# Convolution of the later groups in sixteen 32x32 TensorE tiles, with their loads, writes and reads in a new order

## The chip, the cores and the metric

One core of a Trainium2 chip runs the whole program. The metric is the device time in microseconds; the kernel before takes 413.99 us (median of three runs, 413.82 to 414.37). The engines of the core work side by side: TensorE (PE, with its weight loads as PEld) multiplies, VectorE (DVE) and ScalarE (ACT) work element by element, GpSimd (POOL) and SyncE (SP) mostly issue DMAs.

## What is computed

The input `x` has 8 sequences of 4160 tokens with 192 channels. First comes a causal convolution over 7 tokens, with softmaxed taps, one set for each of 8 heads of 24 channels. Then an RWKV channel mix: two blends of each token with the one before it, a hidden layer of 1024 with a squared relu, and a sigmoid gate.

```python
w = softmax(weight)                                   # (8 heads, 7 taps)
y[b, s, h, :] = sum over k of w[h, k] * x[b, s - 6 + k, h, :]      # zeros before the start

xk = mu_k * y + (1 - mu_k) * y_prev
xr = mu_r * y + (1 - mu_r) * y_prev                   # y_prev: one token earlier
k  = maximum(xk @ w_k, 0)                             # 192 -> 1024
out = sigmoid(xr @ w_r) * ((k * k) @ w_v)             # float32
```

## The kernel before

**Pairs, steps, bundles.** The eight sequences are worked on in four pairs. A pair runs through steps of 512 tokens (both sequences of a pair lie side by side on the partitions, 64 channels of one and 64 of the other, so three slices cover 192 channels). A step of 512 has eight slots of hidden work; four slots are a bundle, so a step takes two bundles. The first pair has bundles 0 to 15, the second 16 to 31, the third 32 to 47, the fourth 48 to 63, and the last 64 tokens of all sequences are gathered in bundle 64.

**The body of a bundle** (`bundle_rest`, line 861) is an order written out by hand. TensorE gets the k multiplies of two slots, a third slot, the r multiplies of a quad of tokens (`r`, line 594), half of the v multiplies (`v_rows`, line 625), the fourth slot, then the convolution units of the bundle, if it has any, and the other half of v. ScalarE evicts: relu of each slot (`k_relu`, line 549), sigmoid of r (line 605), casts of the convolution (line 319). VectorE squares the relu (line 563), blends (`diff`, `scale`, `add_y`), and multiplies v by r (`v_out`, line 641). All PSUM tiles come from one ring of four buffers of two banks each: each new tile takes the buffer of the fourth tile before it, and its first write waits until that tile has been read.

**The convolution ahead of it.** It is computed some bundles before its tokens are needed, in groups of blocks. `toe` is a banded 128x128 matrix for each head. Groups 0 to 3 of the first pair have a route of their own (`on_pe`). From group 4 on, a group has 10 blocks (the last one of a pair 8), each of 56 tokens on each of two partition halves, and a halo: `load_x` (line 116) brings 64 rows per half, batch and block with DMAs on POOL's queue, which cast to bf16. `conv_tiles` (line 288) multiplies two heads at a time: a 64x64 part of `toe` for input half i and output half j, eight multiplies of 5 x 2 x 24 = 240 columns (192 with 8 blocks) into one PSUM tile. `conv_tiles_out` (line 310) casts the tile to the y tile in SBUF, in one or two pieces. Four such units make a group, two units in each of two bundles, two bundles apart: `xs = [fb - 9] * 2 + [fb - 7] * 2` (line 694), where `fb` is the bundle of the step that needs the group first. So from bundle 15 to bundle 53 every second bundle has two units.

**Turning it.** At the end of the second of these bundles `y_write` (line 416) writes the y tile to HBM in four DMAs on SP's queue, and two bundles later `y_read` (line 429) reads the group back with one transposing DMA into `yT`, channels on partitions. `diff` of the step needs it in bundle `fb - 2`. SP's queue also carries the output, two DMAs per quad, and works in order: an instruction that waits holds up those behind it.

**Buffers.** x tiles (`xb`) rotate through three buffers of 10 blocks, y tiles through two, output tiles through three, `yT` through two (one for each pair in work). `x_tile` (line 103) puts a memset of one element on VectorE ahead of a load, so that POOL's DMA can't start before its place in VectorE's order.

Of the kernel before, what the change touches and what calls it, by code (L numbers as in the profile page):

```python
# [7 lines left out]
FP32 = mybir.dt.float32  # L8
BF16 = mybir.dt.bfloat16
# [5 lines left out]
def kernel(  # L15
# [11 lines left out]
    nc = tc.nc  # L27
# [11 lines left out]
    GB = 10  # L39
    HB = 56  # L40
    NROW = -(-S // (2 * HB)) * 2 * HB
    BANK = 512
# [46 lines left out]
    for p in range(NPAIR):  # L89
        base = 0  # L90
        for nb, s, on_pe in (
            ((3, 0, True), (4, 1, True), (4, 2, True), (5, 3, True), (10, 4, False), (10, 6, False))
            if p == 0
            else ((10, 0, False), (10, 2, False), (10, 4, False), (8, 6, False))
        ):
            groups.append((p, base, nb, first_bundle[first_step[p] + s], on_pe))
            base += nb * (BLK if on_pe else 2 * HB)
        assert S <= base <= NROW


    xbs = {}

    def x_tile(g):
        p, base, nb, _, on_pe = groups[g]
        xb = three.tile([P, GB, 2, D], BF16, tag="xb", name="xb")
        xbs[g] = xb
        if g > 4:

            nc.vector.memset(xb[0:1, 0, 0, 0:2], 0.0)  # L109
        if base == 0:  # L110
            nc.gpsimd.memset(xb[0:32, 0, :, :], 0.0)  # L111
        if not on_pe and base + 2 * nb * HB > S:
            n0 = nb - (base + 2 * nb * HB - S) // HB - 1
            nc.gpsimd.memset(xb[Q:P, n0:nb, :, :], 0.0)

    def load_x(g):
        p, base, nb, _, on_pe = groups[g]
        xb = xbs[g]
        if on_pe:
            parts, step, rows = ((0, base),), BLK, P  # L120
        else:
            parts, step, rows = ((0, base), (Q, base + nb * HB)), HB, Q
        for s in range(2):
            b = 2 * p + s
# [98 lines left out]
    def softmax():  # L223
        nc.vector.tensor_reduce(out=w_max, in_=w_raw, axis=mybir.AxisListType.X, op=ALU.max, negate=True)
        nc.scalar.activation(out=w_exp, in_=w_raw, func=AF.Exp, bias=w_max, accum_out=w_sum)
        nc.scalar.preload_act_table(AF.Sigmoid)
        xbs[0] = three.tile([P, GB, 2, D], BF16, tag="xb", name="xb")
        for c in range(NC):
            cs = slice(c * Q, (c + 1) * Q)
            nc.scalar.copy(out=xbs[0][:, : groups[0][2], :, cs], in_=x_f32[:, :, :, cs])  # L230
        nc.vector.reciprocal(out=w_sum, in_=w_sum)
# [78 lines left out]
    def conv_tiles_out(g, c):  # L310

        m = groups[g][2] // 2
        ps = conv_ps.pop((g, c))
        y = ys[g]
        c0, c1 = 2 * c * G, 2 * (c + 1) * G
        cuts = [c0] + [a for a in range(Q, D, Q) if c0 < a < c1] + [c1]
        for a, b in zip(cuts, cuts[1:]):
# [11 lines left out]
                ),  # L329
            )  # L330

    def conv_units(g):
# [83 lines left out]
    def y_write(g):  # L416
        p, base, nb, _, _ = groups[g]
        if base == 0:
            new_yT(p)
        m = nb // 2  # L420
        for j in range(2):
# [6 lines left out]

    def y_read(g):
        p, base, nb, _, _ = groups[g]  # L430
        r0, r1 = base, min(base + 2 * nb * HB, S)
        nc.sync.dma_start_transpose(
            out=yTs[p][:, :, YC + r0 : YC + r1], in_=y_drams[p][r0:r1, :]
        )
# [244 lines left out]
    def at(table, b, fn, *a):  # L679
        table.setdefault(b, []).append((fn, a))  # L680
# [7 lines left out]
    for g, (p, base, nb, fb, on_pe) in enumerate(groups):  # L688
        if g < 3:
            continue  # L690
        if p == 0:
            xs = {3: [1, 1], 4: [2, 2, 3, 3], 5: [4, 4, 5, 5]}[g]
        else:
            xs = [fb - 9] * 2 + [fb - 7] * 2
        for i, b in enumerate(xs):
            xt.setdefault(b, []).append((g, i))
        if not on_pe:
            at(late, xs[-1], y_write, g)

            at(mix_c if g == 4 else late, xs[-1] + (1 if g < 6 else 2), y_read, g)  # L700
# [55 lines left out]
    def prologue():  # L756
# [14 lines left out]
        nc.vector.memset(w_nrm, 0.0)  # L771
        nc.vector.memset(ones6, 1.0)
        x_tile(1)
        load_x(1)
# [86 lines left out]
    def bundle_rest(b, ns):  # L861
# [42 lines left out]
        for u in units:  # L904
            conv_tiles(*u)
            conv_tiles_out(*u)
        v_rows(*quad, 1)
# [85 lines left out]
```

## Time and profile before

The profiled execution has a span of 412.2 us from its first to its last instruction; the runs' median of 413.99 us is measured around it.

| What | Value |
|---|---|
| Median of three runs | 413.99 us |
| Span of the profiled execution | 412.2 us |
| Mean granted TensorE clock | 1.000 |
| k multiplies (line 537): busy | 191.0 us, x1632 |
| v multiplies (line 625): busy | 188.2 us, x4032 |
| r multiplies (line 594): busy | 43.1 us, x780 |
| convolution multiplies (line 302): busy | 16.6 us, x448 |
| relu on ScalarE (line 549): busy | 253.1 us, x260 |
| sigmoid on ScalarE (line 605): busy | 53.3 us, x65 |
| convolution casts on ScalarE (line 319): busy | 50.7 us, x84 |
| DMA moved | 65.58 MB, mean 159 GB/s |

Busy time is a share of the whole span and hides that stages have different limits; multiplies overlap each other, so the busy times of the groups of TensorE add up to more than the engine's own. What a multiply costs is read better from when the next one starts. The chain of waits is followed back from the last instruction: for each piece it gives start, length, engine, tile and line. The waits view tells for each engine what ended its idle time. A view of windows counts the instructions that overlap each stretch of time.

### The profile page before, as it was taken

The numbers are of one execution on the slowest core, as the hardware profiler recorded it, in microseconds if no ns is written. First come the engines' busy times: TensorE is split into PE (matmuls) and PEld (weight loads), VectorE is DVE, ScalarE is ACT, GpSimd is POOL, SyncE is SP. The second block draws the span as 40 slices with busy tenths as digits, with TensorE's granted clock in tenths as the row PEclk, the third lists the DMA queues.
The fourth block names the chain that finished last, engine by engine and source line by source line (L and its number), as shares of the span: only waits on it lengthen the run. The fifth ranks groups of instructions, "written<-read, shape, count | busy, mean of one in ns | idle before, by whom it ended". The sixth has DMA issues, their size and how long they took to land.

```text
span 412.2 us, 16799 instructions
## 1 busy us (share of the span) xinstructions
PE 403.7 (98%) x7349; PEld 301.7 (73%) x7350; DVE 370.5 (90%) x672; ACT 353.2 (86%) x426; POOL 64.1 (16%) x100
## 2 busy tenths in 40 slices
PE   7899999999999999999999999999999999999996
PEld 5567767767867777776777777777777777777795
DVE  5999799999999998999999999999989898999973
ACT  6899978889988888988888899888889888787781
POOL 8622023022040201104040110304000000000000
PEclk9999999999999999999999999999999999999999
DMA  9999989959978894998769697897863926321223
GB/s 141 192 200 194 191 200 190 253 133 194 198 110 211 151 214 118 200 218 113 198 121 229 156 196 182 111 226 130 188 163 100 184 82 175 107 67 53 80 80 115
DMA packets 137241, 65.58 MB, mean 159 GB/s; under 512 B 87356, under 2 KB 137168, under 8 KB 137168
## 3 DMA queue, kind: packets, MB, share of 16 engines
q1 hardware_dynamic: 95840, 48.42, 44.9%
q0 software_dynamic: 40528, 15.53, 33.0%
q8 instruction: 57, 0.93, 0.9%
q10 hardware_dynamic: 800, 0.57, 0.4%
q14 instruction: 16, 0.13, 0.1%
HBM read 31.62 MB, written 37.09 MB: 167 GB/s over the span
## 4 chain that ended last, share of the span: by engine, by line
PE 88%; DMA 4%; DVE 3%; ACT 2%; issue 1%; POOL 1%; SPq 0%; POOLq 0%
PE ps_v L625 39%; PE ps_k L537 37%; PE ps_r L594 7%; PE ps_c L302 3%; DMA yT<-y_dram 2%; DMA wk<-in_moe_w_k_dram 2%; DVE k L563 1%; PE ps_v L577 1%; DMA y_dram<-y 1%; ACT k_sb L549 1%; ACT y L319 0%; DVE d L480 0%; POOL xb L136 0%; DVE xr L511 0%; SPq L424 0%
## 5 line engine op out<-in xcount | busy, mean ns | idle before, releaser
L549 ACT ACTIVATE k_sb<-ps_k 128x1024 bf16<-128x1024 f32 x260 | 253.1, 1037 | 36.1 <-PE ps_k L537 35.2
L563 DVE TENSOR_TENSOR k<-k_sb 128x1024 bf16<-128x1024 bf16 x260 | 172.6, 685 | 28.3 <-ACT k_sb L549 27.9
L537 PE MATMUL ps_k<-xk,wk 64*128 64x512 bf16 (+1 forms) x1632 | 191.0, 367 | 1.2 <-DMA wk<-in_moe_w_k_dram 0.7
L625 PE MATMUL ps_v<-wv,k 64*128 64x192 bf16 x4032 | 188.2, 243 | 0.2 <-DVE k L563 0.2
L625 PEld LDWEIGHTS <-k 64*128 64x128 bf16 x4032 | 167.7, 94 | 13.6 <-issue 4.0
L537 PEld LDWEIGHTS <-wk 64*128 64x128 bf16 x1632 | 79.9, 94 | 59.6 <-DMA wk<-in_moe_w_k_dram 0.9
L136 POOL DMA_DIRECT2D xb<-in_x_dram x62 | 45.1, 738 | 171.2 <-issue 81.8
L641 DVE TENSOR_TENSOR o_sb<-ps_v,r_sb 128x768 f32<-128x768 f32 x64 | 60.8, 951 | 2.6 <-issue 2.4
L605 ACT ACTIVATE r_sb<-ps_r 128x768 bf16<-128x768 f32 x65 | 53.3, 821 | 10.6 <-PE ps_v L625 9.9
L319 ACT CAST y<-ps_c 128x960 bf16<-128x960 f32 (+5 forms) x84 | 50.7, 685 | 0.0
L594 PEld LDWEIGHTS <-xr 64*128 64x128 bf16 x780 | 34.5, 94 | 15.2 <-issue 1.0
L594 PE MATMUL ps_r<-wr,xr 64*128 64x192 bf16 x780 | 43.1, 243 | 0.5 <-DVE o_sb L641 0.5
L511 DVE TENSOR_SCALAR xr<-d,mu 128x512 bf16<-128x512 bf16 (+1 forms) x102 | 35.1, 348 | 0.0
L480 DVE TENSOR_TENSOR d<-yT 128x1536 bf16<-128x1536 bf16 (+4 forms) x36 | 31.3, 870 | 2.0 <-ACT yT L381 1.1
L511 DVE TENSOR_SCALAR xk<-d,mu 128x512 bf16<-128x512 bf16 (+1 forms) x99 | 32.0, 352 | 0.1
L517 DVE TENSOR_TENSOR xr<-xr,yT 128x1536 bf16<-128x1536 bf16 (+1 forms) x33 | 31.0, 938 | 1.1
L517 DVE TENSOR_TENSOR xk<-xk,yT 128x1536 bf16<-128x1536 bf16 (+3 forms) x33 | 30.4, 921 | 0.1
L302 PEld LDWEIGHTS <-toe 64*64 64x64 bf16 x448 | 9.6, 106 | 11.7 <-issue 10.7
L302 PE MATMUL ps_c<-xb,toe 64*64 64x240 bf16 (+1 forms) x448 | 16.6, 265 | 0.2 <-ACT k_sb L549 0.2
L464 POOL COPY y_tail<-yT 128x195 bf16<-128x195 bf16 x4 | 3.2, 796 | 64.9 <-DMA yT<-y_dram 64.8
L111 POOL MEMSET xb<- 32x384 bf16 x3 | 1.2, 407 | 45.2 <-DVE xb L109 39.2
L371 PEld LDWEIGHTS <-xb 128*32 128x32 bf16 (+3 forms) x264 | 5.3, 119 | 1.9 <-ACT xb L230 1.1
(57 smaller groups left out, 63.0 us busy)
## 6 DMA issues: line engine op xcount, KB each, us to landing
out_dram<-o_sb SPq DMA_DIRECT2D x128, 192.0 KB
xb<-in_x_dram POOLq DMA_DIRECT2D x40, 240.0 KB, 8.2
y_dram<-y SPq DMA_DIRECT2D x44, 210.0 KB
y_dram<-y SPq DMA_DIRECT2D x12, 168.0 KB
xb<-in_x_dram POOLq DMA_DIRECT2D x10, 192.0 KB, 5.5
xb<-in_x_dram POOLq DMA_DIRECT2D x6, 216.0 KB, 4.9
xb<-in_x_dram POOLq DMA_DIRECT2D x6, 144.0 KB, 5.3
wk<-in_moe_w_k_dram POOLq DMA_DIRECT2D x4, 192.0 KB, 7.1
```

The source lines that it names most:

```text
L136: nc.gpsimd.dma_start(out=xb[q0 : q0 + rows, lo:hi, s, :], in_=bass.AP(tensor=x.tensor, offset=x.offset + (b * S + t0 + lo * step) * D, ap ...
L302: nc.tensor.matmul(out=banks[j * Q : (j + 1) * Q, i, :, :, k * G : (k + 1) * G], lhsT=toe[q, h, q], rhs=xbs[g][q, j * m : (j + 1) * m, :, ...
L319: nc.scalar.copy(out=bass.AP(tensor=y.tensor, offset=y.offset + d, ap=[y.ap[0], [m * 2 * D, 2], [2 * D, m], [Q, 2], [1, b - a]],), in_=bas ...
L511: nc.vector.tensor_scalar(out=t[:, c, :L], in0=diffs[s][:, c, :L], scalar1=mu[:, i, c : c + 1], scalar2=None, op0=ALU.mult)
L517: nc.vector.tensor_tensor(out=o, in0=o, in1=y_of(s, sl, 0), op=ALU.add)
L537: nc.tensor.matmul(out=ps[:, i, f * L : (f + 1) * L], lhsT=wk[r, c, fs], rhs=xk[r, c, :L], start=c == 0 and f == 0, stop=c == NC - 1 and f ...
L549: nc.scalar.activation(out=k_sb, in_=ps.rearrange("p a b -> p (a b)"), func=AF.Relu)
L563: nc.vector.tensor_tensor(out=o, in0=i, in1=i, op=ALU.mult)
L594: nc.tensor.matmul(out=ps[:, i, k * D : (k + 1) * D], lhsT=xr[q, c, ts], rhs=wr[q, c, :], start=c == 0, stop=c == NC - 1,)
L605: nc.scalar.activation(out=r_sbs[s, j], in_=r_ps.pop((s, j))[:, :, 0 : 2 * D], func=AF.Sigmoid)
L625: nc.tensor.matmul(out=v_ps[s, j][:, bank, k * D : (k + 1) * D], lhsT=k2s[s][q, f, t * P : (t + 1) * P], rhs=wv[q, f, :], start=half == 0 ...
L641: nc.vector.tensor_tensor(out=o_sb.rearrange("p (b t) d -> p b (t d)", b=2), in0=v_ps.pop((s, j)), in1=r_sbs.pop((s, j)), op=ALU.mult,)
```

## The change

From the middle of the second pair on, the convolution's groups are replaced by larger ones: group 8 takes the second half of the second pair, groups 9 and 10 the third pair, groups 11 and 12 the fourth. Such a group has 20 blocks of 26 tokens on each of four partition quarters (32 rows with the halo), 2080 tokens in all. `conv_sparse` multiplies, for each of two heads, with the 32x32 part of `toe` on the diagonal of input quarter i into output quarter j: 32 multiplies of 240 columns into two PSUM tiles, which it takes from the ring together; each quarter i has a bank of its own, and j takes every fourth block. A group has four such units, now one unit in a bundle. The two PSUM tiles are cast to two y tiles, so that a group holds both y buffers.

The x tiles come from two buffers of 20 blocks; the groups 0 to 3, 4 and 5, and 6 and 7 share one each. A sparse group is loaded in two calls, one per batch, the second with a memset of its own on VectorE ahead of it (`tie_x`). Its writes are eight DMAs in one go, after the fourth unit; it is read back in two halves.

| Group | tokens of its pair | loads at bundles | units in bundles | write | reads |
|---|---|---|---|---|---|
| 8 | 2080 to 4159 | 9, 13 | 15, 16, 17, 18 | 18 | 20, 22 |
| 9 | 0 to 2079 | 17, 19 | 21, 22, 24, 25 | 25 | 27, 30 |
| 10 | 2080 to 4159 | 22, 24 | 27, 29, 31, 33 | 33 | 35, 38 |
| 11 | 0 to 2079 | 29, 32 | 35, 37, 39, 41 | 41 | 43, 46 |
| 12 | 2080 to 4159 | 37, 40 | 43, 45, 47, 49 | 49 | 51, 54 |

Group 7's read ends at token 2080, where group 8 begins.

```diff
+    TB = 26
+    TG = 20
...
-            else ((10, 0, False), (10, 2, False), (10, 4, False), (8, 6, False))
+            else ((10, 0, False), (10, 2, False), (TG, 4, None))
+            if p == 1
+            else ((TG, 0, None), (TG, 4, None))
         ):
+            if on_pe is None:
+                base = min(base, S - nb * 4 * TB)
             groups.append((p, base, nb, first_bundle[first_step[p] + s], on_pe))
...
+    def tie_x(g, s):
+        nc.vector.memset(xbs[g][0:1, 1, s, 0:2], 0.0)
...
-        xb = three.tile([P, GB, 2, D], BF16, tag="xb", name="xb")
+        first = g if g in sparse else (0, 4, 6)[(g > 3) + (g > 5)]
+        if g == first:
+            homes[g] = two.tile([P, TG, 2, D], BF16, tag="xb", name="xb")
+        n0 = sum(grp[2] for grp in groups[first:g])
+        xb = homes[first][:, n0 : n0 + nb, :, :]
...
-    def load_x(g):
+    def load_x(g, batches=range(2)):
...
+        elif g in sparse:
+            parts, step, rows = [(32 * i, base + i * nb * TB) for i in range(4)], TB, 32
...
+    def conv_sparse(g, c):
+        nb = groups[g][2]
+        m = nb // 4
+        if c == 0:
+            ys[g] = [two.tile([P, GB, 2 * D], BF16, tag="y", name="y") for _ in range(2)]
+        tiles = [ring.tile([P, 2, BANK], FP32, tag="k", name="ps_c") for _ in range(2)]
+        xb = xbs[g].rearrange("p (m j) s c -> p j m s c", j=4)
+        for k in range(2):
+            h = 2 * c + k
+            for i in range(4):
+                q = slice(32 * i, 32 * i + 32)
+                banks = tiles[i // 2][:, i % 2, 0 : m * 4 * G].rearrange("p (m s c) -> p m s c", m=m, s=2)
+                for j in range(4):
+                    nc.tensor.matmul(
+                        out=banks[32 * j : 32 * j + 32, :, :, k * G : (k + 1) * G],
+                        lhsT=toe[q, h, q],
+                        rhs=xb[q, j, :, :, h * G : (h + 1) * G],
+                        start=True,
+                        stop=True,
+                    )
+        for y, ps in zip(ys[g], tiles):
+            cast_tiles(y, ps, m, c)
...
+        if g in sparse:
+            m = nb // 4
+            for half in range(2):
+                for j in range(4):
+                    nc.sync.dma_start(
+                        out=bass.AP(
+                            tensor=y_drams[p].tensor,
+                            offset=y_drams[p].offset + (base + (2 * half * nb + j) * TB) * 2 * D,
+                            ap=[[2 * D, TB], [4 * TB * 2 * D, 2 * m], [1, 2 * D]],
+                        ),
+                        in_=ys[g][half][32 * j : 32 * j + TB, :, :],
+                    )
+            return
...
-    def y_read(g):
-        p, base, nb, _, _ = groups[g]
-        r0, r1 = base, min(base + 2 * nb * HB, S)
+    def y_read(g, part=slice(0, 1), of=1):
+        p, base = groups[g][:2]
+        n = (ends[g] - base) // of
+        r0, r1 = base + part.start * n, base + part.stop * n
...
         else:
-            xs = [fb - 9] * 2 + [fb - 7] * 2
+            xs = {8: [15, 16, 17, 18], 9: [21, 22, 24, 25]}.get(g, [fb - 13, fb - 11, fb - 9, fb - 7])
...
+        if g in sparse:
+            at(late, max(fb - 5, xs[-1] + 2), y_read, g, slice(0, 1), 2)
+            at(late, fb - 2, y_read, g, slice(1, 2), 2)
+            b, b1 = {8: (9, 13), 9: (17, 19), 10: (22, 24)}.get(g, (fb - 19, fb - 16))
+            at(early, b, x_tile, g)
+            at(early, b, load_x, g, (0,))
+            b = b1
+            at(early, b, tie_x, g, 1)
+            at(early, b, load_x, g, (1,))
+            continue
...
         for u in units:
-            conv_tiles(*u)
-            conv_tiles_out(*u)
+            if u[0] in sparse:
+                conv_sparse(*u)
+            else:
+                conv_tiles(*u)
+                conv_tiles_out(*u)
```

`cast_tiles` is the old body of `conv_tiles_out`, with the y tile, the PSUM tile and the number of blocks as arguments.

## The prediction

> **What bounds the kernel now.** I read the busy shares first, then the waits of TensorE, then the chain that ended last.
>
> ```profile
> PE 403.7 (98%) x7349; PEld 301.7 (73%) x7350; DVE 370.5 (90%) x672; ACT 353.2 (86%) x426; POOL 64.1 (16%) x100
> ...
> PEclk9999999999999999999999999999999999999999
> ```
>
> TensorE is busy for 98% of 412.2 us and its clock is granted in full. In the list of its waits no entry exceeds 1.5 us, and the few there are lie in the first 60 us; nothing interrupts it later. So an instruction less on TensorE is time, unless the next engine takes over. The chain gives the price of a bundle with and without convolution (start, length, what):
>
> ```profile
> 142.93 0.65 PE ps_k L537 x6
> 143.58 0.45 PE ps_c L302 x16
> 144.03 1.43 PE ps_v L625 x32
> 145.46 1.94 PE ps_k L537 x18
> ...
> 151.19 1.94 PE ps_k L537 x18
> ...
> 154.96 0.65 PE ps_k L537 x6
> 155.61 0.53 PE ps_c L302 x16
> 156.14 1.43 PE ps_v L625 x32
> 157.57 1.94 PE ps_k L537 x18
> ...
> 161.97 1.32 PE ps_v L625 x32
> 163.29 1.72 PE ps_k L537 x15
> ```
>
> The sixteen convolution multiplies of a bundle take 0.53 us and lengthen the v rows behind them from 1.32 to 1.43: 0.64 together for ten blocks (240 columns). For eight blocks (192 columns) it is 0.45 + 0.11 = 0.56. The multiplies started by a given moment, counted in growing windows of line 302, show how these 0.64 are made up:
>
> ```profile
> 155.50:155.55 0.05, 0.01 (x4) 1.00 0.63 148
> 155.50:155.65 0.15, 0.11 (x4) 1.00 0.65 152
> 155.50:155.70 0.20, 0.16 (x8) 1.00 0.64 150
> 155.50:155.80 0.30, 0.26 (x12) 1.00 0.70 164
> 155.50:155.90 0.40, 0.36 (x16) 1.00 0.74 173
> ```
>
> Four start together, then four more every 0.10 us: four rounds of the four 64x64 tiles. 0.64 - 4 x 0.10 = 0.24 us is the change of tile shape, in and out. With 192 columns the counts 8, 12, 16 are reached at 131.62, 131.70, 131.78, so a round is 0.08, and 0.56 - 0.32 gives the same 0.24.
>
> **The change, part by part.** *Removed:* groups 8 to 17, that is 20 bundles with sixteen 64x64 multiplies, fourteen of them at 0.64 and six at 0.56. *Added:* five groups of four units, 20 bundles with 32 multiplies in 32x32 tiles, all with 240 columns (5 blocks x 2 batches x 24). Sixteen tiles make two rounds instead of four. No row shows a 32x32 tile. The streaming of a round I take as before, 0.10, since the columns are the same; the 0.24 as before, since the shape still changes twice; new is that sixteen starts no longer come "together". Lower bound for one start: the four in 155.536 to 155.549 lie within 0.013 us, 0.003 each. Upper bound: the 85 one-column multiplies of line 782, in 32-column tiles, of which 30 have started 0.22 us after the first and 61 after 0.47, so 0.008 each. The nearest row is the first (the same data, at the same place in the bundle): 15 x 0.003 = 0.05. A unit then costs 0.24 + 0.20 + 0.05 = 0.49, which saves 0.15 in fourteen bundles and 0.07 in six: 2.10 + 0.42 = **2.5 us**. At 0.008 the starts bind (31 x 0.008 + 0.10 + 0.24 = 0.59): 14 x 0.05 - 6 x 0.03 = 0.5 us. At 0.002, 0.47: 2.9 us.
>
> Here a rule speaks against the change: the Trainium skill, TensorE: Matmul & The Clock Gate, section "Wait — 56ns, not 53.3ns?", says that matmuls never start closer than about 25 ns, however few columns they have. By it 31 starts would take 0.78, a unit 1.12, and the kernel would lose 14 x 0.48 + 6 x 0.56 = 10 us. The windows above show four starts within 0.013 us, so at least over different tiles the rule doesn't hold. The same page, section "Part 3: Packing small matmuls — row/col tiling", reports sixteen 32x32 tiles at 10.6 times one tile's rate and 4 ns per further tile, which no row of this trace shows; 15 x 0.004 would give 0.50 for a unit.
>
> *ScalarE.* The casts stay 84; eighteen of 256, 512 and 768 elements become 320, 640 and 960 (392, 599, 812 to 444, 706, 973 ns): 1.9 us more in all, spread over bundles where ScalarE has idle time, hence free, except in the following place.
>
> ```profile
> 151.88 2.86 ACT L549 ACTIVATE k_sb<-ps_k 128x1024 bf16<-128x1024 f32 x3 [0.82 <-PE ps_k L537]
> 154.60 0.83 ACT L605 ACTIVATE r_sb<-ps_r 128x768 bf16<-128x768 f32 x1
> 155.64 1.02 ACT L549 ACTIVATE k_sb<-ps_k 128x1024 bf16<-128x1024 f32 x1 [0.21 <-PE ps_k L537]
> 156.56 1.88 ACT L319 CAST y<-ps_c 128x960 bf16<-128x960 f32 x3
> ```
>
> In a bundle with units ScalarE is full: from 151.88 it is free again at 158.30 (the next relu's start), 6.42 us, while TensorE needs 157.57 - 151.19 = 6.38, and will need 6.23. Before, each such bundle is followed by one without units (0.82 idle), which absorbs this. After, units stand in bundles 15 to 18, 21, 22, 24, 25 and then every second one up to 49: bundles 16, 18, 22 and 25 follow a unit bundle and hold a sigmoid. Their first relu comes 158.30 - (151.88 + 6.23) = 0.19 late, so does the sigmoid, and the second new PSUM tile reuses the sigmoid's buffer (ring of four). The sigmoid now ends at 155.43, the ninth multiply would start 0.03 after 155.54, and the signal takes some 0.06: slack 0.08, so 0.11 of stall, four times: **0.4 us lost**. The new unit takes both PSUM tiles at its start, where the old one took the second a round later; with r done this early, that alone costs nothing in the other bundles. If ScalarE isn't late the loss is 0; if the heavier units (two pairs of 444 + 706) add to it, 0.9.
>
> *DVE.* Thirteen small memsets of 59 ns before, thirteen after (eight tiles, five ties); DVE has 0.4 us free in a unit bundle (5.98 of 6.38). Free; without that cover 13 x 0.06 = 0.8.
>
> *Loads.* POOL issues the same 640 rows per DMA (738 ns each), eight per group in two calls of four, two to four bundles apart. Its three waits for ps_c (line 114, 6.3 us) go, since these memsets go; the copy of the tail is queued behind loads in the same way. The latest load starts two whole bundles (12 us) ahead of the one with its convolution, against 8.2 us to landing plus 2.9 us for four issues. Free; uncovered, it would cost what lies over 12 us. In the first twelve bundles only the waits of POOL for freed buffers change (one of 0.6 us ahead of group 4), and no one on the chain waits for it.
>
> *Writes and reads.* Writes and reads keep their numbers (56 and 14) and nearly their rows, but each sparse group is written in one go of eight, and out's DMAs wait behind on SP for 8 x 0.74 instead of 4 x 0.74 us (2.94 for four). Three output buffers cover 12 us. Reads come in two halves; the shortest lead is that of group 8's first half, from bundle 20 to the diff in 22, some 10 us against 6.88 from issue to landing on the chain. Free; late, DVE's diff would wait, then the xk of the next step and all of TensorE.
>
> Sum: 2.5 - 0.4 = 2.1 us off the 412.2 us span. The median, 413.99, lies 1.8 us over the span, and I leave that distance: **411.9 us**.
>
> **The rivals.**
> 1. *The gain is eaten* (starts of 8 ns, or ScalarE late in every unit bundle). For it: ScalarE's 6.42 against 6.23; against it: every second bundle gives 0.82 back. 0.5 us less 0.4 of stall: 413.9.
> 2. *Slower: the tiles don't run sixteen at once*, but, say, four, as in the rounds now. Place: line 364's 32 multiplies. Eight rounds cost 0.24 + 0.80 = 1.04 a unit: 14 x 0.40 + 6 x 0.48 = 8.5 us, 422.5. It decides once a unit costs over 0.66 (with no stall left then): 14 x 0.02 + 6 x 0.10 = 0.9. Against it: four column tiles stream together in line 371's multiplies and two row tiles in line 625's. Eight at once gives 0.64 and 414.5, no change.
> 3. *Slower through the y buffers.* A sparse group holds both, so the first cast of the next waits for the writes. From the last cast's end (7.1 us into its bundle, 158.30 - 151.19) to the next group's first (5.4 into the second bundle after) there are 12.0 + 5.4 - 7.1 = 10.3 us, in the handovers 25-27, 33-35 and 41-43. Four writes took 6.55 on the chain (36.07 to 42.62); eight, 2.9 more: 9.5. If eight took twice four's, 13.1, each handover would lose 2.8 on a full ScalarE: 8.4 - 2.1, 420.3. It decides above 10.3 + 0.7 us.
> 4. *More:* no stall and starts at 2 ns: 411.1.
>
> **How the numbers follow.** Forecast (411.5 to 412.9): 0.57. Rival 4: 0.08. Rival 1 and eight at once (413.2 to 414.6): 0.18. Rival 2: 0.08. Rival 3: 0.09. The likeliest gives the time. The range 411.0 to 414.4 takes in the forecast, rival 4 and most of rival 1, and leaves rivals 2 and 3 out. A measurement of this kernel can tell about 0.2%, 0.83 us, from no change; faster are the forecast and rival 4, 0.65, the same rival 1, 0.18, slower 0.17.
>
> **What would show it.** Right: in windows of the new unit's line, sixteen starts within some 0.06 us and sixteen more 0.10 to 0.13 us later; chain pieces of ps_c plus the lengthened v rows near 0.49 where it was 0.64; alternating bundles near 11.95 instead of 12.10; short waits of TensorE for ScalarE's r_sb in bundles 16, 18, 22, 25. Wrong: counts that grow in fours or eights; waits of ScalarE's casts for y_dram writes; waits of DVE's diff for yT; a granted clock below full.

## The result and the profile after

The changed kernel takes 413.82 us (median of 17 runs, 412.28 to 417.62), the kernel before 414.05 us beside it (17 runs, 413.26 to 415.01). The ratio is 1.0002, with a 95% interval of 0.9984 to 1.0020: no change. 411.9 had been forecast. Ratios and intervals, here and below, leave out runs that lie more than 1.5% above the fastest of the same kernel; medians and ranges take in every run. The runs of the changed kernel spread over 5.3 us, those of the kernel before over 1.8. The profiled execution of the changed kernel took 415.07 us, with a span of 413.4 us against 412.2; it is one of the longer runs, and the sums below are its own, not those of the median.

The page, in the lines that answer to those shown of before (busy shares, granted clock):

```profile
PE 402.0 (97%) x7669; PEld 302.3 (73%) x7670; DVE 370.8 (90%) x672; ACT 354.6 (86%) x426; POOL 57.4 (14%) x91
...
PEclk9999999999999999999999999999999999999999
```

320 multiplies more, and yet 1.7 us less busy time on TensorE; the span is 1.2 us longer. So TensorE has saved time, and stood still for longer than it saved.

**The saving.** The chain of the changed kernel (start, length, what) in two bundles with a unit, the second directly behind the first:

```profile
163.41 0.35 PE ps_c L364 x32
163.77 1.43 PE ps_v L681 x32
165.19 2.00 PE ps_k L593 x18
...
169.65 0.58 PE ps_c L364 x32
170.23 1.43 PE ps_v L681 x32
171.65 1.94 PE ps_k L593 x18
```

The first unit takes 0.35 us and lengthens the v rows from 1.32 to 1.43: 0.46 together, where the old one took 0.64 or 0.56. The second takes 0.23 longer. Windows of line 364 in the same two units (length, busy time and count of TensorE, of weight loads, clock, DMA share, GB/s) show why:

```profile
163.30:163.40 0.10, 0.06 (x16) 0.06 (x18) 1.00 0.95 138
163.30:163.46 0.16, 0.12 (x18) 0.12 (x32) 1.00 1.02 137
163.30:163.55 0.25, 0.21 (x32) 0.19 (x32) 1.00 1.08 131
...
169.55:169.70 0.15, 0.12 (x8) 0.11 (x9) 1.00 1.16 305
169.55:169.85 0.30, 0.27 (x15) 0.13 (x15) 1.00 1.13 314
```

Sixteen tiles start within 0.05 us, the next sixteen from 0.11 to 0.16 us after the first: all sixteen work side by side. In the unit at 169.6 eight have started and the ninth, first into the second PSUM tile, waits until 169.8 for ScalarE. This happens in four units (at 113.6, 125.7, 149.8 and 169.6 us, that is bundles 16, 18, 22 and 25), which end 0.15, 0.22, 0.15 and 0.22 us later than the others.

**The loss.** First the chain around bundle 22:

```profile
141.02 0.59 SPq L705
141.61 0.04 issue
141.65 10.01 DMA yT<-y_dram
...
151.69 0.96 DVE d L536
...
155.04 0.67 PE ps_r L650 x12
```

The read of group 8's first half is issued at 141.65 and has landed at 151.66; the diff has by then waited 2.60 us. TensorE stands 1.34 us for what DVE does after it: in bundle 23, r waits for v_out (start, length, in brackets its wait).

```profile
151.59 2.11 PE L593 MATMUL ps_k<-xk,wk 64*128 64x512 bf16 x18
155.04 0.67 PE L650 MATMUL ps_r<-wr,xr 64*128 64x192 bf16 x12 [1.34 <-DVE o_sb L697]
...
158.82 2.12 PE L593 MATMUL ps_k<-xk,wk 64*128 64x512 bf16 x18
```

From its first k multiply to that of bundle 24, bundle 23 takes 7.23 us, where a bundle without a unit takes 5.73: the late read costs 1.50. Second, a unit at 205.9 us (windows of line 364 again):

```profile
205.90:206.20 0.30, 0.26 (x21) 0.15 (x21) 1.00 0.09 9
205.90:207.15 1.25, 0.39 (x21) 0.15 (x21) 1.00 0.58 184
205.90:207.30 1.40, 0.48 (x32) 0.25 (x32) 1.00 0.64 204
```

21 of 32 multiplies have started by 206.2, and not one more until 207.15. The profile names no releaser for this wait ("PE ps_c L364 <- issue"): every operand is there, but TensorE is without instructions.

Balance of the profiled execution, in us against the kernel before, from the lengths of the bundles: units -3.12 (14 x 0.18 + 6 x 0.10), late ScalarE +0.75, late read +1.50, bundle 31 with the stand at 206 us +1.23, bundles 30, 38 and 39 +0.61 (0.29, 0.14 and 0.18; their cause comes with T3 below), an earlier start -0.36: +0.6. TensorE's last multiply ends 0.95 later, at 409.30 against 408.35; the 0.3 left over lie in bundles that are each longer by 0.16 or less, and weren't traced.

### The profile page after: what moved, and what is told of

Its sections match the earlier page's. It is cut to its first block, busy times and chain, and to the rows that moved or that the text cites. A ratio compares the mean times of both kernels' runs of the same rounds, so it can differ in the third digit from the quotient of the medians.

```text
span 413.4 us, 17417 instructions
## 1 busy us (share of the span) xinstructions
PE 402.0 (97%) x7669; PEld 302.3 (73%) x7670; DVE 370.8 (90%) x672; ACT 354.6 (86%) x426; POOL 57.4 (14%) x91
## 4 chain that ended last, share of the span: by engine, by line
PE 81%; DVE 8%; DMA 6%; ACT 2%; issue 1%; SPq 1%; DVEq 0%; ACTq 0%
PE ps_v L681 36%; PE ps_k L593 34%; PE ps_r L650 7%; DMA yT<-y_dram 4%; DVE k L619 2%; PE ps_c L364 2%; PE ps_v L633 1%; DVE d L536 1%; DMA y_dram<-y 1%; DVE o_sb L697 1%; ACT k_sb L605 1%; DMA x_f<-in_x_dram 1%; DVE xk L567 1%; DVE xk L573 1%; DVE xr L567 1%
## 5 line engine op out<-in xcount | busy, mean ns | idle before, releaser
L593 PEld LDWEIGHTS <-wk 64*128 64x128 bf16 x1632 | 83.6, 94 | 56.8 <-issue 2.5
L154 POOL DMA_DIRECT2D xb<-in_x_dram x62 | 44.2, 721 | 147.9 <-DVE xb L113 68.1
L337 ACT CAST y<-ps_c 128x960 bf16<-128x960 f32 (+2 forms) x84 | 52.7, 707 | 0.5 <-PE ps_c L364 0.5
L364 PEld LDWEIGHTS <-toe 32*32 32x32 bf16 x640 | 4.3, 87 | 9.8 <-issue 8.5
L364 PE MATMUL ps_c<-xb,toe 32*32 32x240 bf16 x640 | 9.5, 267 | 0.9 <-issue 0.9
```

The source lines that it names most:

```text
L154: nc.gpsimd.dma_start(out=xb[q0 : q0 + rows, lo:hi, s, :], in_=bass.AP(tensor=x.tensor, offset=x.offset + (b * S + t0 + lo * step) * D, ap ...
L337: nc.scalar.copy(out=bass.AP(tensor=y.tensor, offset=y.offset + d, ap=[y.ap[0], [m * 2 * D, 2], [2 * D, m], [Q, 2], [1, b - a]],), in_=bas ...
L593: nc.tensor.matmul(out=ps[:, i, f * L : (f + 1) * L], lhsT=wk[r, c, fs], rhs=xk[r, c, :L], start=c == 0 and f == 0, stop=c == NC - 1 and f ...
```

## The experiments

Three theories: **T1**, the read comes late; **T2**, units in consecutive bundles make ScalarE late; **T3**, TensorE's program comes late. For T3 the trace has one more row. TensorE's program reaches it in DMA packets of 16 KB (queue q8 of the page, "instruction": 57 packets before; 60 after, 0.98 MB for some 15,340 multiplies and weight loads, 64 bytes each, so a packet is 256 of them). Counted are TensorE's instructions (multiplies, weight loads and the few that only wait for a semaphore) that have started when packet n starts to move, less 256 n: its "lateness" in instructions. It is -93 to -78 at the earliest; that is probably about when a packet is asked for. After 60 us four packets of the changed kernel are over 90 late, 29, 30, 36 and 37 (104, 112, 147 and 105), and TensorE stops in each of the four at the same place, 193 instructions into a packet, for 0.32, 1.15, 0.17 and 0.15 us: these are bundles 30, 31, 38 and 39 of the balance.

**1. Group 9's loads out of the way of group 8's writes.**

```diff
-            b, b1 = {8: (9, 13), 9: (17, 19), 10: (22, 24)}.get(...
+            b, b1 = {8: (9, 13), 9: (14, 16), 10: (22, 24)}.get(...
```

> Group 9 is loaded at bundles 14 and 16 instead of 17 and 19; all else as in the changed kernel. T1 (the tiles bring about 3 us, and 2.2 of it are given back in bundle 22, where DVE's diff waits for the first half of group 8, whose eight writes crawl because group 9's second load moves data at the same time): the writes of group 8 land before 138 us instead of about 142, the read is issued before 138 instead of at 141.65, the diff's wait for yT (2.6 us) falls under 0.5, and the median goes from 413.8 to about 411.8. T2 (the loss comes from units standing in consecutive bundles and ScalarE): loads change nothing, 413.8. T3 (TensorE now and then isn't given its instructions in time, as at 206 us): the waits for yT may go but the median stays above 413 with runs spread over 4 us or more.

Measured: 417.21 us (415.65 to 420.06), ratio 1.0081 [1.0053, 1.0109]. The diff of bundle 22 doesn't wait any more, but this doesn't speak for T1: the read is issued at 142.62, not before 138 (it stands in SP's order behind bundle 20's outputs, whatever the writes do), and the diff starts 9.8 us after it, at 152.40, because TensorE is 3.4 us later by then. The time went up by 3.4 us. In the windows of all engines there is a stand of 2.6 us in the unit at 120.6 (length, then busy time and count of TensorE, its weight loads, DVE, ScalarE, POOL):

```profile
120.00:122.00 2.00, 0.86 (x21) 0.24 (x18) 2.00 (x5) 1.50 (x2) 0.00 (x0) 1.00 1.39 218
122.00:124.00 2.00, 0.80 (x31) 0.66 (x32) 0.89 (x3) 0.43 (x1) 0.00 (x0) 1.00 1.31 239
```

Packet 17 starts at 120.7 us, when TensorE has already stopped, 193 instructions late, takes 1.28 us, and TensorE goes on at 123.2.

**2. Group 10's loads one bundle later.** `10: (23, 25)` in the same line.

> Group 10 is loaded at bundles 23 and 25 instead of 22 and 24; all else as in the changed kernel. T1: the read of group 8's first half is still issued near 141.6, but lands without group 10's load beside it at about 148 to 149 instead of 151.6; the diff waits 0 to 1 us instead of 2.6; median about 412.4. T2: 413.8. T3: above 413, spread as before.

Measured: 412.74 us (411.34 to 413.93, 12 runs), ratio 0.9968 [0.9953, 0.9983]: faster than the kernel before, and than the changed one (whose interval, 0.9984 to 1.0020, doesn't meet this one); T1 had 412.4. The diff (start, length, in brackets its wait):

```profile
150.89 0.96 DVE L536 TENSOR_TENSOR d<-yT 128x1536 bf16<-128x1536 bf16 x1 [1.05 <-DMA yT<-y_dram]
```

2.60 us of waiting have become 1.05 with nothing done but taking group 10's load from beside the read, which lands 8.7 us after its issue instead of 10.0. The 1.05 left cost TensorE nothing: bundle 23 is back to 5.73 us.

```profile
152.41 2.11 PE L593 MATMUL ps_k<-xk,wk 64*128 64x512 bf16 x18
...
158.14 2.11 PE L593 MATMUL ps_k<-xk,wk 64*128 64x512 bf16 x18
```

T3 had expected more than 413.

**3. Group 8 earlier.** Group 7's units at 10, 10, 11, 11, group 8's at 13, 15, 16, 17, its loads at 8 and 10; its write and first read follow one bundle earlier.

```diff
-            xs = {8: [15, 16, 17, 18], ...
+            xs = {8: [13, 15, 16, 17], ...
```

> Group 8's units move from bundles 15 to 18 to 13, 15, 16, 17, its write to 17 and its first read to 19, three bundles ahead of the diff that needs it instead of two (group 7's units go to 10 and 11, and group 8's loads to 8 and 10, to make place). T1: the diff's wait for yT in bundle 22 goes although the writes still share the DMA engines with group 9's loads; median about 411.8. T2: as many consecutive unit bundles as before, 413.8. T3: above 413, spread as before.

Measured: 414.64 us (413.0 to 417.36), ratio 1.0015 [0.9996, 1.0035]. The read is issued at 134.96 and the diff's wait is gone; stands of 0.88 us at 146.2 and 0.84 at 173.2 have come.

**4. All three moves.**

> The three moves together: group 8's units and write one bundle earlier, group 9's loads at 14 and 16, group 10's at 23 and 25. T1: no wait of a diff for yT anywhere after 100 us; median 411.3 to 411.8, about what the prediction gave. T2: 413.8. T3: above 413, and runs spread over 4 us as before.

Measured: 416.29 us (412.29 to 419.18), ratio 1.0037 [1.0011, 1.0063]. No late read in bundle 22, but a stand of 2.03 us at 113.7. The four together: the late read is real, and it goes when group 10's load isn't beside it (2) or when it is issued a bundle earlier (3 and 4); 3 and 4 pay for it with stands. T2 alone would have left all four at 413.8.

**5. The program shifted.** Experiment 1 with 64 one-column multiplies more in the warming, half a packet.

```diff
-    SHORT = 85
+    SHORT = 149
```

> The kernel with group 9's loads at 14 and 16 (417.2 us, with TensorE standing still for 2.6 us in a unit at 120.6), and 64 more one-column multiplies in the warming at the start: 128 more TensorE instructions, half of a 16 KB piece of program, ahead of everything; every DMA and every other instruction stays where it is. T3 (TensorE's next piece of program arrives late when the DMA engines are full, and the 64 instructions of a unit use the rest up in 0.4 us): pieces and units meet at other places, so the stand at 120.6 changes by more than 1 us or is gone, others may appear, and the median differs by over 1 us from 417.2. T1 and T2 (waits for data or ScalarE): the same stands at the same units, 417.2 plus at most 0.5 us for the multiplies themselves.

Measured: 421.32 us (420.29 to 424.24), ratio 1.0186 [1.0153, 1.0219]. The stand at 120 us is now 3.46 us long, and TensorE stops in k multiplies, not in a unit; new ones are at 114.1 (0.44) and 164.4 (0.65). Before 75 us the shift costs 2.8 us, more than the 0.5 allowed for: there are two more stands at the same place in a packet, 2.69 us at 11.7 (packet 2, 193 late) and 0.80 at 19.7. Another 3.1 come near 120 us. So the stand depends on where in the program the packets end, as T3 says, and the burst of a unit isn't needed for it.

**6. Group 9's loads spread**, two DMAs at each of bundles 14 to 17, in experiment 1's kernel; each pair gets a memset of its own ahead of it.

```diff
...
+    SPREAD = {9: (14, 15, 16, 17)}
...
+                for n, bn in enumerate(SPREAD[g]):
+                    if n > 0:
+                        at(early, bn, tie_x, g, n // 2, n % 2 * Q)
+                    at(early, bn, load_x, g, (n // 2,), slice(n % 2 * 2, n % 2 * 2 + 2))
```

> The same kernel (417.2 us) without the extra multiplies; group 9's eight load DMAs are issued two at a time at bundles 14, 15, 16, 17 instead of four at a time at 14 and 16. T3: the program's pieces are fetched between the loads, the latest start of a piece falls from 0.75 of a piece late to under 0.5, the stand of 2.6 us at 120.6 goes, median 412 to 414. If the stand had another cause than the crowd of loads: 417 as before. T1's wait for yT in bundle 22 stays away in either case.

Measured: 416.86 us (414.98 to 419.01), ratio 1.0064 [1.0043, 1.0085]. A miss: instead of one stand there are three, 0.57 at 108.0, 1.12 at 114.7, 1.58 at 121.6. Packet 17 is 156 instructions late instead of 193, but packet 16 is now 136 late instead of 84.

**7. All loads spread** (the table of the expectation).

> All five sparse groups' loads two DMAs at a time in four bundles (group 8 at 9 to 12, 9 at 15 to 18, 10 at 23 to 26, 11 at 29 to 32, 12 at 37 to 40); units, writes and reads as in the changed kernel. T1 and T3 together: neither the wait for yT at 150 us (under 0.5) nor a stand over 0.5 us; median 411.3 to 412.2, runs within 2 us. T3 wrong: stands stay, 413 and more.

Measured: 418.57 us (415.78 to 421.57), ratio 1.0107 [1.0068, 1.0146]: a clear miss. The wait for yT is down to 0.3 us, but at 94.1 us, in an old 64x64 unit, TensorE stands for 3.38 us. The windows of all engines:

```profile
94.00:96.00 2.00, 0.34 (x9) 0.17 (x9) 1.74 (x4) 1.94 (x3) 0.00 (x0) 1.00 1.67 172
96.00:98.00 2.00, 0.55 (x8) 0.19 (x8) 0.00 (x0) 0.00 (x0) 0.00 (x0) 0.75 1.18 274
98.00:100.00 2.00, 2.00 (x30) 1.88 (x28) 0.00 (x0) 0.96 (x1) 0.00 (x0) 0.50 0.52 165
100.00:102.00 2.00, 2.00 (x24) 1.14 (x22) 1.30 (x3) 0.66 (x1) 0.00 (x0) 0.89 0.74 187
```

The third number from the end is the granted clock: towards the end of the stand it falls to 0.50, for 3.4 us (the windows' 0.75, 0.50 and 0.89 make 1.0, 2.0 and 0.4 us at half speed). TensorE works for 3.0 of these, which costs about another 1.5 us. The DMA view of 86 to 95 us, in 40 slices, shows what moved before packet 13, which starts at 94.9:

```profile
DMA  9560004999999999999999999999999999999999
GB/s 83 44 23 24 24 20 76 278 291 291 290 286 160 77 82 77 80 80 79 80 79 75 85 80 78 81 79 79 86 82 85 81 113 225 170 115 115 130 133 259
```

From 87.6 to 89 us a transposing read moves 290 GB/s, from then to 93 us 80 GB/s with the DMA engines just as full; in that stretch 17 to 48 packets of a spread load each microsecond move beside it. That they slow the read is argued from this one place, not shown.

**8. As 7, with groups 8 and 12 writing in two halves a bundle apart.**

```diff
...
-                at(late, xs[-1], y_write, g)
+                at(late, xs[-1], y_write, g, *([(0,)] if g in (8, 12) else []))
+                if g in (8, 12):
+                    at(late, xs[-1] + 1, y_write, g, (1,))
```

> As the one with all loads spread, and groups 8 and 12 write four DMAs after their last unit and four a bundle later, so that the outputs wait less on SP's queue and the first read doesn't stand behind all eight writes. T1: read of group 8's first half issued before 139 us instead of at 141.65; 411.3 to 412.0. If the first read waits for the second half's writes too, it is issued later than before, and bundle 22 loses 1 to 3 us: 413 to 415.

Measured: 419.53 us (418.75 to 424.1), ratio 1.0164 [1.0120, 1.0209]: a miss too. The same stand, now at 95.7, and seven in all.

**9 and 10. A shorter read.** Only what bundle 22's diff needs (528 tokens) is read in bundle 20, the rest of the half in 21; 9 in the changed kernel, 10 in experiment 2's.

```diff
-            at(late, max(fb - 5, xs[-1] + 2), y_read, g, slice(0, 1), 2)
+            if g == 8:
+                at(late, 20, y_read, g, slice(0, 33), 130)
+                at(late, 21, y_read, g, slice(33, 65), 130)
+            else:
+                at(late, max(fb - 5, xs[-1] + 2), y_read, g, slice(0, 1), 2)
```

> The changed kernel, with the first read of group 8 (1040 tokens, bundle 20) cut in two: 528 tokens in bundle 20, all that the diff of bundle 22 needs, and 512 in bundle 21. Loads, units and writes stay. T1 (1040 tokens take 10.0 us from issue to landing, and only 7.4 us lie between the issue behind bundle 20's outputs and the diff): half the tokens land 1.5 to 3 us sooner, the diff's wait falls from 2.6 to under 1.2, median 412.0 to 412.8. If the landing is late whatever its size (an engine or queue is taken by something else until then): 413.8 as before.

> The kernel with group 10's loads at 23 and 25 (412.74 us, wait of 1.1 us left), with the same cut of the read. T1: no wait of the diff for yT over 0.3 us in bundle 22; median 411.6 to 412.2. Otherwise 412.7.

Measured: 9 gave 411.70 to 421.33 us over 12 runs, median 416.94 (ratio 1.0027 [0.9998, 1.0057], from seven of them); 10 gave 412.94 (411.53 to 414.78), ratio 0.9967 [0.9949, 0.9985]. In both the diff of bundle 22 waits no more (it starts at 149.2 and 149.4), so T1's mechanism holds; but bundle 23 takes 5.73 us in 10 as in 2, so there was nothing left to gain, and a stand of 0.78 us at 244.4 has come. The profiled execution of 9, its slowest (421.33 us, outside the ratio), has an accident that shows how far a crowd reaches; it explains that execution alone. SP's queue (start, time until the next):

```profile
146.12 3.41 SPq L488 DMA_TRANSPOSE yT<-y_dram  x1
149.63 1.11 SPq L705 DMA_DIRECT2D out_dram<-o_sb  x2
150.78 13.68 SPq L488 DMA_TRANSPOSE yT<-y_dram  x1
164.56 7.15 SPq L705 DMA_DIRECT2D out_dram<-o_sb  x6
```

Group 10's load runs beside the third read; SP comes free 13.7 us later, the outputs behind it are late, DVE waits 6.9 us for an output buffer, and TensorE stands for 4.10 us at 171.5 (its packet 25 late as well) and 2.44 at 175.8; from 176 to 184 us the granted clock is 0.50 to 0.69. Both medians miss what T1 alone expected.

**11 and 12. Experiment 2 shifted** by a quarter and by half a packet.

```diff
-    SHORT = 85
+    SHORT = 53       (12: SHORT = 21)
```

> The kernel with group 10's loads at 23 and 25, and 32 one-column multiplies fewer in the warming: 64 TensorE instructions, a quarter of a piece of program, fewer ahead of everything; DMAs as they are. T3: the starts of the pieces' fetches move against the loads; the latest (0.41 to 0.5 of a piece late at 196 and 243 us) change by more than 0.1, stands over 0.3 us come or go, and the median moves by 0.5 us or more either way. Without T3: 412.7 or up to 0.3 less.

> As before with 64 one-column multiplies fewer: half a piece. T3: again other starts and stands, a median that differs by 0.5 us or more from that with 85 multiplies or from that with 53. Without T3: 412.7 or up to 0.5 less.

Measured: 415.94 us (415.05 to 418.18, ratio 1.0055 [1.0034, 1.0076]) and 413.19 (412.07 to 415.57, ratio 0.9985 [0.9965, 1.0005]). The expected spread is there, but for 11 not for the expected reason: it has lost 2.5 us by 73 us, in a stand of 2.28 at 10.1 us, and nothing more after it. That the shift acts through packets holds (the stand begins 193 instructions into a packet, as the others do); that it acted on the changed part of the schedule doesn't.

**13. Loads and reads pulled apart**, from experiment 2's kernel.

```diff
-            at(late, fb - 2, y_read, g, slice(1, 2), 2)
+            at(late, fb - 1 - (g == 8), y_read, g, slice(1, 2), 2)
-            b, b1 = {8: (9, 13), 9: (17, 19), 10: (23, 25)}.get(g, (fb - 19, fb - 16))
+            b, b1 = {8: (9, 13), 9: (17, 19), 10: (24, 26)}.get(g, (fb - 19, fb - 15))
```

> The kernel with group 10's loads at 23 and 25 (412.74 us), with loads and reads of the later groups pulled apart: group 10's loads at 24 and 26, second reads of groups 9 to 12 one bundle later (31, 39, 47, 55), second loads of groups 11 and 12 one bundle later (33, 41). T3 with crowds as its cause: the pieces that start 0.41 and 0.5 late at 196 and 243 us start under 0.3 late, no stand over 0.3 us after 190, and the median falls to 411.5 to 412.3. If the lateness doesn't come from reads and loads meeting, the starts stay at 0.4 to 0.5 and the median at 412.7.

Measured: 416.70 us (416.20 to 418.46), ratio 1.0084 [1.0065, 1.0103]. A miss: packets near 199 and 245 us are still 109 and 108 instructions late, and group 10's load at bundle 26 delays group 9's write: ScalarE's cast waits 2.5 us for y_dram.

**14. Only groups 11 and 12 loaded three bundles earlier**, `(fb - 22, fb - 19)`, in experiment 2's kernel.

> The same kernel (412.74 us) with only the loads of groups 11 and 12 moved, three bundles earlier (26 and 29, 34 and 37), so that each load ends before the second read of the group before it begins. T3: as in the run with the reads later, starts under 0.3 late at 196 and 243 us, median 411.5 to 412.3; the first load at 26 falls together with group 9's write and may make a piece late near 170 instead. Otherwise 412.7.

Measured: 422.62 us (421.20 to 425.03), ratio 1.0222 [1.0196, 1.0247]. What it was to improve is hidden by what it brings: the chain (start, length, what) goes through group 9's eight writes.

```profile
177.66 9.22 DMA y_dram<-y
...
187.06 0.97 ACT y L337
...
188.07 1.46 PE ps_k L593 x6
```

The last of the eight lands at 186.9, the casts of the next group wait 5.6 us in two places ("ACT y L337 <- DMA y_dram<-y"), and TensorE stands for 4.26 us at 183.8 and 2.07 at 237.4. This is the third rival of the prediction, with a load as its cause.

**15 and 16. The quarter shift in experiment 13's kernel and in the kernel before.**

> The kernel with loads and reads pulled apart, with 32 one-column multiplies fewer at the start: the shift that cost 3.2 us in the kernel with group 10's loads late (415.94 against 412.74). If pulling apart takes away what makes pieces late, the shift matters little: within 1 us of the unshifted one. If it only moved the meeting points, the shift costs again 2 us or more.

> The kernel before, with 32 one-column multiplies fewer at the start, nothing else. T3: its pieces have started at most 0.45 late, with 32 instructions in a unit's burst instead of 64; the shift moves them, but stands stay short: 413.5 to 415, against 3.2 us for the same shift in the changed schedule. If the shift itself (less warming) costs the time, the kernel before loses 3 us as well: 417.

Measured: 421.53 us (420.48 to 423.21, ratio 1.0192 [1.0170, 1.0213]) and 417.44 us (417.35 to 418.08, ratio 1.0092 [1.0079, 1.0105]). The second decides: the kernel before loses 3.4 us too, all of it by 59 us; the windows of all engines:

```profile
10.00:12.00 2.00, 0.00 (x0) 0.00 (x0) 0.83 (x2) 0.17 (x1) 1.57 (x3) 1.00 1.55 191
12.00:14.00 2.00, 1.21 (x21) 0.83 (x22) 0.02 (x1) 0.56 (x1) 0.93 (x1) 0.67 1.30 201
14.00:16.00 2.00, 2.00 (x22) 1.43 (x19) 1.93 (x5) 1.02 (x1) 1.68 (x3) 0.50 1.56 190
```

In the stage of the weights' loads TensorE stands 3.0 us for the first packet, and the clock halves. After 60 us the kernel before has no stand over 0.33 us, in either place of its program. So its later stages weren't exposed in these two places, and the changed ones are; 15 can't be read, since it has the early stand as well (3.17 us).

**17 and 18. The change taken out of the second pair (17), and out of the second and third (18).** The other groups stay as before; one of their two-unit bundles moves to make place (17: group 9 at 19, 19, 20, 20 and the first sparse group in 22 to 25; 18: group 13 at 35, 35, 36, 36 and the first sparse group in 38 to 41).

```diff
-            else ((10, 0, False), (10, 2, False), (TG, 4, None))
-            if p == 1
+            else ((10, 0, False), (10, 2, False), (10, 4, False), (8, 6, False))
+            if p == 1          (18: if p < 3)
```

> The second pair keeps the kernel before's groups of ten and eight blocks with 64x64 parts to its end (units 15, 15, 17, 17, 19, 19, 20, 20); only the third and fourth pairs use the 32x32 tiles, the third pair's first group in units 22 to 25, the loads of the next at 23 and 25. Sixteen bundles instead of twenty gain: 16 x 0.18 = 2.9 less six small ones, about 2.4. T1: no wait for yT in bundle 22. T3: stands of up to 1 us as the crowds fall. 411.7 to 412.8 if only T1 had cost the change its time; 413 to 415 if the crowds of the larger groups' loads, writes and reads go on making pieces late.

> Only the fourth pair uses the 32x32 tiles (units 38 to 41 and 43, 45, 47, 49; loads 32, 35 and 37, 40); all ahead of bundle 31 works as in the kernel before. Eight bundles gain, two of them small: about 1.2 to 1.4 us on its own. If the tiles' gain stands wherever the DMAs leave TensorE's program alone, the median is 412.6 to 413.0 and the runs lie within 2 us, as before; if the larger groups bring stands here too, 413.5 and more.

Measured: 17 gave 412.68 us (412.16 to 415.08), ratio 0.9978 [0.9965, 0.9991]; 18 gave 415.02 (413.51 to 416.6), ratio 1.0029 [1.0005, 1.0053]. 17 is the change without group 8: no late read, one stand of 1.06 us at 143.2. Its median equals that of experiment 2. 18 is slower than the kernel before by its interval, and why stays unclear: its profile has no stop 193 instructions into a packet after 60 us, TensorE's last multiply ends 0.24 us before that of the kernel before, but the program ends 4.8 us after it instead of 3.9.

**The stands of TensorE on its program**, the longest of each run that has one, with the instruction in the packet at which it stopped, and the lateness of the packet it waited for:

```
run    at us   stand us   instruction mod 256   lateness of the packet
after  206.1   1.15       193                   112
1      120.6   2.61       193                   193
2      198.4   0.48       193                   105
3      146.2   0.88       193                   69
4      113.7   2.03       193                   166
5      120.2   3.46       193                   193
6      121.6   1.58       193                   156
7       94.1   3.38       193                   193
8       95.7   3.38       193                   193
9      171.5   4.10       193                   193
10     244.4   0.78       193                   156
11      10.1   2.28       193                   155
12      12.1   1.25       193                   157
13     201.3   0.57       193                   109
15      10.3   3.17       193                   193
16       9.8   3.01       193                   193
17     143.2   1.06       193                   137
```

TensorE stops at the same instruction, whichever kernel, place or operation: 193 into a packet (192 are counted in the changed kernel, whose trace has one multiply less than weight loads). The longer stands of 13, 14 and 15 that wait for a load, a write or ScalarE lie elsewhere, at 16, 144, 198, 208 or 211. This is what T3 rests on. From the earliest start of a packet, some 85 instructions ahead, to this stop are 280 instructions; where the packet takes longer to come, TensorE stands until 1.2 to 1.7 us after it has moved. TensorE starts 15,340 instructions in 412 us, so 280 are an estimated 7.5 us. Lateness alone doesn't decide: packet 24 of the kernel before is 114 late and costs nothing, since TensorE gets to the 193rd instruction 2.4 us after its start; in packet 30 of the changed kernel, 112 late, a unit's burst brings it there after 1.5 us.

## Why the prediction was wrong

**The price of the tiles was right, a little too high.** 0.49 per unit was forecast, 0.46 measured, from the terms of the working: change of shape as before, two rounds, starts at 0.003. The upper bound of 0.008 a start and rival 2 (tiles four or eight at a time) are out. The gain is 3.12 us instead of 2.5.

**ScalarE's lateness was right in mechanism and place, too small in size.** Bundles 16, 18, 22, 25, at the ninth multiply, as forecast; 0.15 to 0.22 each instead of 0.11, 0.75 us instead of 0.4, inside the bound of 0.9. Net of both 2.4 us, against 2.1.

**The step that failed is "Writes and reads", put down as "Free".** It held 10 us of lead for group 8's first half against 6.88 from issue to landing. Both were wrong. SP's queue:

```profile
127.70 7.71 SPq L466 DMA_DIRECT2D y_dram<-y  x8
135.51 6.10 SPq L705 DMA_DIRECT2D out_dram<-o_sb  x4
141.65 4.73 SPq L488 DMA_TRANSPOSE yT<-y_dram  x1
```

Bundle 20's outputs stand ahead of the read and wait for DVE's v_out (at 140.09 in the chain), so it is issued at 141.65; the diff was ready at 149.1. That is 7.4 us. And 6.88 was the landing of another read, in the trace of before; this one took 10.0 beside group 10's load, whose four DMAs are issued from 144.99 on, and still 8.7 without it (experiment 2). The prediction had named the diff as what would be late, but had xk wait next, where it was r that waited for v_out; and it didn't set the load of bundle 22 against the read of bundle 20. Price: 1.50 us in bundle 23; in experiment 2 it is gone, and the median lies 1.08 lower, with a stand of 0.48 left elsewhere; 17 avoids the read.

**The second step that failed isn't in the working at all.** "Free" for loads, writes and reads took the DMA engines' users one by one, each against its own deadline. TensorE's program is one more user without a line in the kernel. The lateness of its packets was there to be read before: at most 114 instructions after 60 us, one over 90, and no stop. With the larger groups it goes up to 147, with four over 90, and each of the four stops TensorE: the four bundles are 1.84 us longer, 1.15 of it in one stand. In experiments 1, 5, 7, 8 and 9 a single stand takes 2.6 to 4.1 us. That the wider spread of runs comes from this too is argued, not shown: there is one trace of the changed kernel.

Here a page and the runs differ: the Trainium skill, Runtime: NRT & Kernel Launch, section "Instruction fetch mechanics", has programs fetched in blocks of 256 instructions, as here, and calls the cost of crossing a block mostly hidden. In these runs it is hidden only where the next block has moved 1.2 to 1.7 us before TensorE comes to its 193rd instruction; 17 of the 20 profiled kernels have a stop of 0.48 us or more there.

**Rival 3** (the y buffers) cost nothing in the changed kernel: no cast waits for y_dram. Experiments 13 and 14 show it when a load moves beside the write. **Rival 1** (gain eaten) names the right number, 413.9, by the wrong mechanism.

**What stays open.** What makes a packet late isn't settled. Spread loads made it worse (6, 7), pulled-apart loads and reads no better (13), and a read at 80 GB/s with a few load packets beside it was seen once (7). Nor is the price of the stands over all runs known; the two kernels that keep some of the gain, 0.9 to 1.3 us of the 2.1 forecast (17 and 2, both 412.7), still have a stand each.

## What to carry to other kernels

Where the change makes transfers fewer and larger, set each against every other that moves in the same bundles, and count the issue from where the instruction stands in its queue, behind what that queue waits for. An engine's program is such a transfer too: its packets' starts against the instructions started show how near to a stand a schedule is (with how fast TensorE uses up the rest), and a wait "on issue" always at the same instruction of a packet is its sign. The schedule here answered to moves of loads, reads and the program by 1 us less to 9 us more, so a gain of half a per cent has to be measured with the schedule it comes with.

## What was not expected of the hardware

TensorE stops 193 instructions into a packet of 256 when the next one hasn't come, and resumes 1.2 to 1.7 us after that one has moved. With stands of 3.0 us and more (3.01 in experiment 16, 3.38 in 7, 3.46 in 5, 4.10 in 9) the granted clock falls to 0.50, for 3.4 us (6.8 in 9). The length of the stand doesn't decide alone: the clock falls with 2.28 us in experiment 11 too, and stays at 1.00 with 2.61 in 1 and with the 2.69 at 11.7 us in 5. The Trainium skill, TensorE: Matmul & The Clock Gate, Part 1, has the clock halved after an idle window of about 3.4 us; the runs agree in size, but a stand of 2.28 was enough once. Sixteen 32x32 tiles start within 0.05 us, 0.003 each, as four 64x64 tiles do.
